# Reordering the products, the first loads and the weight sums of a seven-product projection stage

## The chip, the cores and the metric

One Trainium2 chip, one core. The metric is device time of one execution in microseconds (us), lower is better. The kernel before has a median of 1763.17 us over 3 runs, from 1761.24 to 1765.32.

## What is computed

Two independent attention blocks, A (sliding, dilated window) and B (full), each with 2048 rows, width 640 and 32 heads of 20, in float32. The stage around the change is the first product of block A, `x @ wqkv`:

```python
qkv = (x @ wqkv).reshape(B, S, 3, H, Dh)      # x: 1 x 2048 x 640, wqkv: 640 x 1920
# A: each row attends to itself and 7 earlier rows, 2 apart; B: to all rows
# softmax, weighted sum of v, then @ wo; outputs of A and B side by side
```

## The kernel before

Every float32 product is made of three passes on TensorE (PE): each operand is split into a rounded part ("hi", a cast on ScalarE, ACT) and what the rounding left ("lo", a subtraction on VectorE, DVE), and hi x hi, hi x lo and lo x hi are added up in PSUM (`PASSES`, `product`, lines 30 and 397).

**Block A's projection** (`a_steps`, line 687) makes 12 of the 16 row tiles of 128 rows, in six pairs (`ARows`, `XA[0]` to `XA[5]`), against four groups of weight columns of 512, 512, 448 and 448 (`ACols`, `WP[0]` for the first two, `WP[1]` for the last two). The inner size 640 is five chunks of 128.

1. The first pair of pairs, four row tiles, meets column group 0 chunk by chunk, as the chunks arrive from memory: for each k the x chunks are split (`ARows.chunk`), the weight half too (`ACols.half`), and 12 matmuls follow. Then come the same four tiles against column group 1 from weights that are all there, 15 matmuls a tile.
2. All further work is done by `a_quad` (line 426): two row tiles against two column groups at once with seven block products in the place of eight. It needs sums and differences of blocks of x (`ARows.sums`, `second`, addressed by `X.s(n)`) and of blocks of the weights (`ACols.turn`: four DVE operations in place and into the tile `sums`, then two casts and two subtractions; addressed by `W.T(n)`). One quad has 54 matmuls, five PSUM banks of eight in turn (`next_bank`), one copy and adds on ACT and DVE, and four stores to DRAM (`a_store`, three buffers). `XA[0]` and `XA[1]` run it against `WP[1]` first, quads 0 and 1, then `XA[2]` to `XA[5]` against `WP[0]` and `WP[1]` in turn, quads 2 to 9.

**What sets the order.** Each engine runs its instructions in the order in which the program emits them. `a_steps` and `a_quad` are generators: at each `yield` the loop at line 722 counts n up, issues the stores that are due (`tick`) and emits the side work of that n: `WP[1].base` at n = 1, 2; `WP[1].turn` at n = 4, 5; `WP[0].turn` at n = 8, 10; the split of a later pair of x tiles (`base` at n = 12, 16, 24, 32, `sums` and `second` one step later); the copies of weights to DRAM (`keep`); two late weight chunks (`late_w`, loaded at n = 16 and 20, split two steps later); and at n = 9 eight DMAs that write constants to DRAM. Quad 0 has the yields 8 to 11, quad 1 has 12 to 15, quad 2 has 16 to 19. So what n = 8 emits stands on ACT, DVE and the DMA queue of SP (SyncE) between the first and the second section of quad 0. In a quad before the change:

```python
product(b[0], A11, B11, True, True)               # 6 matmuls
act.copy(c[0], b[0])
product(b[1], X.s(2), W.T(2), True, True)         # 6, needs the weight sums
add(c[1], c[0], b[1])
product(b[0], A12 + l1, B21 + W.c[0], False, True)  # 9, into the bank that ACT has read
```

**Loads.** The loads at the head go out from two queues: per chunk, SP issues the weight half and the x chunk of `XA[0]` (128 x 256), and ACT that of `XA[1]`. Each pair's raw x lies in a `vb` tile of which there are two, and the tile `sums` is a third user of them.

Of the kernel before, what the change touches and what calls it, by code (L numbers as in the profile page):

```python
# [9 lines left out]
F32 = mybir.dt.float32  # L10
# [11 lines left out]
KC = 5  # L22
# [43 lines left out]
def attention_pair(ctx, tc, xa, wqk_a, wv_a, wo_a, xb, wqk_b, wv_b, wo_b, oa, ob):  # L66
# [156 lines left out]
    def lo_of(lo, raw, hi):  # L223
        dve.tensor_tensor(lo, raw, hi.bitcast(F32), ALU.subtract)

    class ARows:


        def __init__(self, p):
            self.p = p  # L230
            self.raw = sb.tile([128, KC, 256], F32, tag="vb", bufs=2, name="stg")
            self.rest = None

        def load(self, *ks, e=sp):
            c = slice(self.p * 256, self.p * 256 + 256)
            if ks:
                for k in ks:
                    e.dma_start(self.raw[:, k], xa[k * 128:(k + 1) * 128, c])
            else:
                sp.dma_start(self.raw, xa[:, c].rearrange("(k p) c -> p k c", p=128))  # L240

        def parts(self, u, k, src):
            m = src.shape[1]
            act.copy(u[:, 0, k:k + m], src)
            lo_of(u[:, 1, k:k + m], src, u[:, 0, k:k + m])

# [3 lines left out]
        def chunk(self, k):  # L250
            if self.rest is None:
                self.home()
                self.rest = sb.tile([128, 2, KC // 2, 128], F32R, tag="raw", bufs=2, name="xr")
            if k == KC - 1:
                self.parts(self.u, 6, self.raw[:, k].rearrange("p (t c) -> p t c", t=2))
                return
            self.parts(self.u, k, self.raw[:, k:k + 1, :128])
            self.parts(*((self.u, 4 + k // 2) if k % 2 else (self.rest, k // 2)), self.raw[:, k:k + 1, 128:])

# [14 lines left out]
        def second(self):  # L274
            self.parts(self.u, 8, self.raw[:, :KC - 1].rearrange("p k (t c) -> p (k t) c", t=2))

# [9 lines left out]
    class ACols:  # L286


        def __init__(self, P):
            self.P, self.n = P, AC[2 * P + 1] - AC[2 * P]  # L290
# [18 lines left out]
            self.raw = [sb.tile([128, 2, n], F32, tag=tag, bufs=2 * (P + 1), name="wr") for tag, _ in self.tags for _ in range(2)]  # L309
            self.raw.append(sb.tile([128, 2, n], F32, tag=f"big{2 + P}", bufs=1, name="wr"))  # L310
            self.lo = []
# [7 lines left out]
        def load(self, k, js=range(2)):  # L319
            P = self.P  # L320
            if P == 0:
                for j in js:
                    sp.dma_start(self.raw[k][:, j].rearrange("p (m c) -> p m c", c=128),
                                 wqk_a[4 * j:4 * j + 4, :, k].rearrange("m p c -> p m c"))
                return
            r = self.raw[k].rearrange("p j c -> p (j c)")
            sp.dma_start(r[:, :256].rearrange("p (m c) -> p m c", c=128), wqk_a[8:10, :, k].rearrange("m p c -> p m c"))
            for h in range(2):
                sp.dma_start(r[:, 256 + h * 320:576 + h * 320], wv_a[h, :, k])

# [17 lines left out]

        def turn(self, kp, x):

            ev, od = self.raw[2 * kp:2 * kp + 2]
            x = x[:, :, :self.n]
            dve.tensor_tensor(x[:, 0], ev[:, 1], ev[:, 0], ALU.subtract)
            dve.tensor_tensor(x[:, 1], od[:, 1], ev[:, 1], ALU.subtract)
            dve.tensor_tensor(od[:, 1], od[:, 1], x[:, 0], ALU.subtract)
            dve.tensor_tensor(od[:, 0], od[:, 0], od[:, 1], ALU.subtract)
            self.lo.append([None, None])
            for o, r in ((1, od), (0, x)):
                self.lo[kp][o] = sb.tile([128, 2, self.n], F32R, tag=self.tags[kp][0], bufs=self.tags[kp][1], name="wl")
                act.copy(self.t[kp][o], r)  # L360
                lo_of(self.lo[kp][o], r, self.t[kp][o])
# [64 lines left out]
    def a_quad(X, W):  # L426
# [10 lines left out]
        act.copy(c[0], b[0])  # L437
        product(b[1], X.s(2), W.T(2), True, True)
        add(c[1], c[0], b[1])
        product(b[0], A12 + l1, B21 + W.c[0], False, True)  # L440
        a_store(g, t, act.copy, b[0])
        yield
        product(b[2], X.s(1), W.T(1), True, True)
        add(c[1], c[1], b[2])
        product(b[3], X.s(4) + l1, B22 + W.c[1], True, True)
        a_store(g + 1, t, add, c[1], b[3])
        yield
        product(b[1], X.s(3), W.T(3), False, True)
        add(c[0], c[0], b[1])
        product(b[4], A22 + l2, W.T(4) + W.c[0], True, True)  # L450
        a_store(g, t + 1, add, c[0], b[4])
        yield
        product(b[2], l2, W.c[1], False, True)
        a_store(g + 1, t + 1, add, c[0], b[2])
        yield
# [12 lines left out]

    XA = [ARows(p) for p in range(2)]
    WP = [ACols(0), ACols(1)]  # L470
    for k in range(KC):
        WP[0].load(k, (0,))
        XA[0].load(k)
        XA[1].load(k, e=act)
    for k in range(KC):
# [246 lines left out]
    for n, _ in enumerate(a_steps()):  # L722
        tick()
        if n == 0:
            for j in range(2):
                WP[1].half(KC - 1, j)
        elif n in (1, 2):
            WP[1].base(n - 1)
        elif n == 3:
            sums = sb.tile([128, 2, 512], F32, tag="vb", bufs=2, name="sums")  # L730
        elif n in (4, 5):
            WP[1].turn(n - 4, sums)
        elif n in (8, 10):
            WP[0].turn(n // 2 - 4, sums)
        if n in (5, 12, 14, 21):
# [4 lines left out]
        elif n in (13, 17, 25, 33):  # L740
            XA[n // 8 + 1].sums()
            XA[n // 8 + 1].second()
        if n == 9:
            for c in range(4):
                sp.dma_start(kb_d[c, 2 * DH:].rearrange("t h (s c) -> (t h) s c", c=128),
                             neg.unsqueeze(1).to_broadcast([64, 4, 128]))
            for u in (ka_d, va_d):
                for hf in range(2):
                    sp.dma_start(u[hf, :PAD].rearrange("p (b c) -> p b c", c=128),
                                 zero.unsqueeze(1).to_broadcast([PAD, KC, 128]))  # L750
        if n in (3, 4) or n > 9 and n % 2 and keeps:
            P, k, j = keeps.pop(0)
            WP[P].keep(k, j)
        if n in (16, 20):
            k = n // 2 - 8
            late_w = [sb.tile([128, WP[1].n], t, tag="aq", bufs=2, name="wt") for t in (F32, F32R)]
            sp.dma_start(late_w[0][:, :128], wv_a[0, :, k, 192:])
            sp.dma_start(late_w[0][:, 128:], wv_a[1, :, k])
        elif n in (18, 22):
            act.copy(late_w[1], late_w[0])  # L760
            lo_of(late_w[0].bitcast(F32R), late_w[0], late_w[1])
            late_w = [late_w[1], late_w[0].bitcast(F32R)]
        elif n in (19, 23):
            k = n // 2 - 9
            WP[1].b12 = {k // 2: late_w}
            WP[1].keep(k, 1)
# [233 lines left out]
    P = {}  # L1000
# [424 lines left out]
```

## Time and profile before

| | us |
|---|---|
| median of 3 runs | 1763.17 |
| lowest, highest | 1761.24, 1765.32 |
| the profiled execution, its own time | 1762.97 |
| its span (first to last instruction) | 1761.2 |
| PE busy in the span | 1738.2 (99%) |
| DVE, ACT, POOL busy | 1417.0, 1335.5, 1228.7 |

Times in the trace are counted from the start of the span. PE is the matmul engine, PEld its weight loads, SPq and ACTq the DMA issues of SyncE and ScalarE. A row of the timeline gives start, duration (of all that are merged in it), engine, operation, output<-inputs, count, and in brackets the idle time before it with what ended it. Tiles have the program's names: `wr` raw weights, `wc`, `wt` their split parts, `wl` lo parts of the weight sums, `stg` raw x, `xn` and `xr` split x, `sum` the two accumulators of a quad (c[0], c[1]), `ro` a result on its way to DRAM, `ps_st` PSUM.

### The profile page before, as it was taken

What the parts mean: (1) busy time and instruction counts of PE and PEld (TensorE: products, weight loads), DVE (VectorE), ACT (ScalarE), POOL (GpSimd) and SP (SyncE); (2) the same over time, 40 slices, a digit from 0 to 9 for tenths busy, and PEclk for the clock granted to TensorE, in tenths of its full rate; (3) what the DMA queues carried; (4) which work ended last, traced back from release to release, by engine and by line L of the source; (5) the groups of instructions that cost most, each with busy time, mean ns of one, the idle gap of its engine ahead of it and who ended that gap; (6) DMA issues with size and microseconds to landing.
All of it is one profiled execution on the core that took longest, in us unless ns stands there. A gap on an engine that the chain in (4) does not pass through costs nothing.

```text
span 1761.2 us, 32060 instructions
## 1 busy us (share of the span) xinstructions
PE 1738.2 (99%) x11271; PEld 990.1 (56%) x11271; DVE 1417.0 (80%) x1948; ACT 1335.5 (76%) x2605; POOL 1228.7 (70%) x1086
## 2 busy tenths in 40 slices
PE   8999999999999999999999999999999999999999
PEld 7888888774444444444444444544444444444569
DVE  7655323689999999999999999999999999999400
ACT  5223222129899999999999999899999999989881
POOL 0000693595988888888899798988888898745442
PEclk9999999999999999999999999999999999999999
DMA  7567967774536554644474455536542634222123
GB/s 227 177 207 252 332 247 258 247 221 113 160 104 175 148 150 128 159 132 141 149 178 143 122 152 152 160 105 173 151 149 90 159 111 132 60 70 69 55 71 111
DMA packets 221496, 270.19 MB, mean 153 GB/s; under 512 B 92812, under 2 KB 142616, under 8 KB 221336
## 3 DMA queue, kind: packets, MB, share of 16 engines
q1 hardware_dynamic: 220040, 266.85, 50.7%
q8 instruction: 88, 1.44, 0.4%
q10 hardware_dynamic: 1296, 1.31, 0.2%
q14 instruction: 72, 0.59, 0.1%
HBM read 193.33 MB, written 74.74 MB: 152 GB/s over the span
## 4 chain that ended last, share of the span: by engine, by line
PE 84%; POOL 4%; DMA 3%; DVE 2%; ACT 2%; issue 1%; SPq 1%; DVEq 0%; POOLq 0%; ACTq 0%
PE ps_st L61 84%; POOL akv L61 2%; DVE mx L61 2%; ACT e L61 1%; DMA stg<-xb 1%; POOL braw L61 1%; SPq L61 1%; DMA bq<-qb_d 1%; DMA stg<-wv_b 0%; ACT more L61 0%; DMA stg<-wo_a 0%; POOL xn L61 0%; POOL al L61 0%; DMA qb_d<-pr 0%; DMA ot_b<-braw 0%
## 5 line engine op out<-in xcount | busy, mean ns | idle before, releaser
L61 DVE TENSOR_REDUCE mx<-ps_st 128x1 f32<-128x512 f32 (+1 forms) x1500 | 1217.8, 878 | 77.2 <-PE ps_st L61 65.8
L61 ACT ACTIVATE e<-ps_st 128x512 f32<-128x512 f32 x2048 | 1067.0, 608 | 36.2 <-PE ps_st L61 16.1
L61 PE MATMUL ps_st<-bq,bk 62*128 62x512 f32 x2048 | 610.9, 439 | 0.2
L61 PE MATMUL ps_st<-bk,bq 60*128 60x512 f32 x2048 | 557.0, 435 | 4.2 <-DVE mx L61 2.1
L61 PEld LDWEIGHTS ps_st<-bq,bk 62*128 62x128 f32 x2048 | 287.9, 184 | 478.6 <-ACT e L61 336.5
L61 PE MATMUL ps_st<-e,vb 128*32 128x512 f32 x4096 | 542.8, 604 | 2.8 <-DVE mx L61 0.4
L61 POOL TENSOR_TENSOR braw<-braw,more 128x512 f32<-128x512 f32 x224 | 288.3, 1287 | 146.9 <-ACT more L61 141.1
L61 POOL TENSOR_TENSOR akv<-akv 128x640 f32<-128x640 f32 (+3 forms) x304 | 282.9, 931 | 23.8
L61 PEld LDWEIGHTS ps_st<-bk,bq 60*128 60x128 f32 x2048 | 264.8, 184 | 37.9 <-DVE mx L61 13.4
L61 POOL TENSOR_TENSOR akv<-akv,aq 128x1280 f32<-128x1280 f32 x64 | 188.2, 2940 | 25.4 <-DMA akv<-ka_d 25.3
L61 PEld LDWEIGHTS ps_st<-e,vb 128*32 128x32 f32 x4096 | 81.9, 108 | 157.3 <-issue 70.8
L61 POOL TENSOR_TENSOR akv<-akv,al 128x1280 f32<-128x1280 f32 x64 | 152.2, 2378 | 0.2
L61 PE MATMUL ps_st<-wc,xn 128*128 128x512 f32 (+1 forms) x544 | 136.5, 384 | 7.7 <-ACT sum L61 4.8
L61 ACT COPY ro<-ps_st 128x320 f32<-128x320 f32 (+2 forms) x102 | 45.9, 452 | 122.8 <-PE ps_st L61 114.9
L61 ACT COPY more<-ps_st 128x512 f32<-128x512 f32 x224 | 132.6, 592 | 2.2 <-PE ps_st L61 1.4
L61 PE MATMUL ps_st<-ww,xn 128*128 128x320 f32 x768 | 125.8, 314 | 0.5 <-ACT e L61 0.5
L61 PEld LDWEIGHTS ps_st<-ww,xn 128*128 128x128 f32 x768 | 113.5, 188 | 20.8 <-ACT e L61 8.8
L61 PEld LDWEIGHTS ps_st<-wc,xn 128*128 128x128 f32 x544 | 103.9, 191 | 24.4 <-ACT sum L61 5.9
L61 PE MATMUL ps_st<-xn,w 128*128 128x512 f32 x480 | 115.6, 389 | 0.3 <-DVE xn L61 0.3
L61 POOL MEMSET ve<- 128x347 f32 x4 | 1.4, 389 | 159.4 <-DVE ro L61 159.4
L61 PEld LDWEIGHTS ps_st<-xn,w 128*128 128x128 f32 x480 | 90.0, 188 | 19.4 <-DVE xn L61 0.7
L61 ACT CAST pr<-ps_st 128x512 fp32r<-128x512 f32 x40 | 23.5, 588 | 89.6 <-PE ps_st L61 89.6
(89 smaller groups left out, 1121.6 us busy)
## 6 DMA issues: line engine op xcount, KB each, us to landing
akv<-ka_d SPq DMA_DIRECT2D x128, 320.0 KB
akv<-va_d SPq DMA_DIRECT2D x128, 320.0 KB
wx<-wa_d SPq DMA_DIRECT2D x24, 480.0 KB
kb_d<-pr SPq DMA_DIRECT2D x20, 512.0 KB
qb_d<-pr SPq DMA_DIRECT2D x20, 512.0 KB
bk<-kb_d SPq DMA_DIRECT2D x16, 640.0 KB
bq<-qb_d SPq DMA_DIRECT2D x64, 160.0 KB
rb<-s_d SPq DMA_DIRECT2D x128, 64.0 KB
```

The costliest lines, as they stand in the source:

```text
L61: return self.tc.keep_in_program_order(op(*a, **k))
```

## The change

The order of the products in a quad changes: the first product, then `b[3]` and the second part of `b[0]`, which need x sums but no weight sums, then those with `W.T`; `b[4]` comes last. `ACols.turn` is split into `sums` (DVE) and `second` (casts, subtractions), which are emitted one step apart. The first x chunks of `XA[0]` and `XA[1]` come as one 128 x 512 load for each k from SP into one tile, in the space that later holds `WP[1]`'s split weights (`big2`), so the two `vb` tiles are free from the start. In odd chunks the two x blocks are split by one operation on each engine. The constants go to DRAM at n = 33 and 35, and the two late weight chunks are split four steps after their load.

```diff
@@ -226,23 +226,17 @@
     class ARows:
 
 
-        def __init__(self, p):
-            self.p = p
+        def __init__(self, p, raw=None):
+            self.p, self.raw, self.rest = p, raw, None
+
+        def load(self):
             self.raw = sb.tile([128, KC, 256], F32, tag="vb", bufs=2, name="stg")
-            self.rest = None
-
-        def load(self, *ks, e=sp):
-            c = slice(self.p * 256, self.p * 256 + 256)
-            if ks:
-                for k in ks:
-                    e.dma_start(self.raw[:, k], xa[k * 128:(k + 1) * 128, c])
-            else:
-                sp.dma_start(self.raw, xa[:, c].rearrange("(k p) c -> p k c", p=128))
+            sp.dma_start(self.raw, xa[:, self.p * 256:self.p * 256 + 256].rearrange("(k p) c -> p k c", p=128))
 
         def parts(self, u, k, src):
-            m = src.shape[1]
-            act.copy(u[:, 0, k:k + m], src)
-            lo_of(u[:, 1, k:k + m], src, u[:, 0, k:k + m])
+            to = k if isinstance(k, slice) else slice(k, k + src.shape[1])
+            act.copy(u[:, 0, to], src)
+            lo_of(u[:, 1, to], src, u[:, 0, to])
 
         def home(self):
             self.u = big(self.p % 2, [128, 2, 16, 128], "xn")
@@ -254,8 +248,12 @@
             if k == KC - 1:
                 self.parts(self.u, 6, self.raw[:, k].rearrange("p (t c) -> p t c", t=2))
                 return
-            self.parts(self.u, k, self.raw[:, k:k + 1, :128])
-            self.parts(*((self.u, 4 + k // 2) if k % 2 else (self.rest, k // 2)), self.raw[:, k:k + 1, 128:])
+            if k % 2:
+                n = 4 + k // 2
+                self.parts(self.u, slice(k, n + 1, n - k), self.raw[:, k].rearrange("p (t c) -> p t c", t=2))
+            else:
+                self.parts(self.u, k, self.raw[:, k:k + 1, :128])
+                self.parts(self.rest, k // 2, self.raw[:, k:k + 1, 128:])
 
         def base(self):
             self.home()
@@ -272,7 +270,10 @@
             dve.tensor_tensor(a12, a12, a11, ALU.subtract)
 
         def second(self):
-            self.parts(self.u, 8, self.raw[:, :KC - 1].rearrange("p k (t c) -> p (k t) c", t=2))
+            hi, lo = (self.u[:, i, 8:].rearrange("p (k t) c -> p k t c", t=2) for i in range(2))
+            src = self.raw[:, :KC - 1].rearrange("p k (t c) -> p k t c", t=2)
+            act.copy(hi, src)
+            lo_of(lo, src, hi)
 
         def rows(self, t, k):
             if t and k % 2 == 0 and k < KC - 1:
@@ -286,7 +287,7 @@
     class ACols:
 
 
-        def __init__(self, P):
+        def __init__(self, P, end):
             self.P, self.n = P, AC[2 * P + 1] - AC[2 * P]
             n = self.n
             if P == 0:
@@ -307,7 +308,7 @@
                 self.b11, self.odd, self.t, self.e = [], [], [], e
             self.c = [[lambda i, j=j: self.last[j][i]] for j in range(2)]
             self.raw = [sb.tile([128, 2, n], F32, tag=tag, bufs=2 * (P + 1), name="wr") for tag, _ in self.tags for _ in range(2)]
-            self.raw.append(sb.tile([128, 2, n], F32, tag=f"big{2 + P}", bufs=1, name="wr"))
+            self.raw.append(end)
             self.lo = []
 
         def home(self, kp):
@@ -323,10 +324,16 @@
                     sp.dma_start(self.raw[k][:, j].rearrange("p (m c) -> p m c", c=128),
                                  wqk_a[4 * j:4 * j + 4, :, k].rearrange("m p c -> p m c"))
                 return
-            r = self.raw[k].rearrange("p j c -> p (j c)")
-            sp.dma_start(r[:, :256].rearrange("p (m c) -> p m c", c=128), wqk_a[8:10, :, k].rearrange("m p c -> p m c"))
-            for h in range(2):
-                sp.dma_start(r[:, 256 + h * 320:576 + h * 320], wv_a[h, :, k])
+            r = self.raw[k]
+            sp.dma_start(r[:, 0, :256].rearrange("p (m c) -> p m c", c=128), wqk_a[8:10, :, k].rearrange("m p c -> p m c"))
+            if k < KC - 1:
+                r = r.rearrange("p j c -> p (j c)")
+                for h in range(2):
+                    sp.dma_start(r[:, 256 + h * 320:576 + h * 320], wv_a[h, :, k])
+                return
+            sp.dma_start(r[:, 0, 256:], wv_a[0, :, k, :192])
+            sp.dma_start(r[:, 1, :128], wv_a[0, :, k, 192:])
+            sp.dma_start(r[:, 1, 128:], wv_a[1, :, k])
 
         def one(self, u, raw):
             act.copy(u[0], raw)
@@ -346,7 +353,7 @@
             self.one(self.b11[kp], self.raw[2 * kp][:, 0])
             self.one(self.odd[kp], self.raw[2 * kp + 1])
 
-        def turn(self, kp, x):
+        def sums(self, kp, x):
 
             ev, od = self.raw[2 * kp:2 * kp + 2]
             x = x[:, :, :self.n]
@@ -354,8 +361,11 @@
             dve.tensor_tensor(x[:, 1], od[:, 1], ev[:, 1], ALU.subtract)
             dve.tensor_tensor(od[:, 1], od[:, 1], x[:, 0], ALU.subtract)
             dve.tensor_tensor(od[:, 0], od[:, 0], od[:, 1], ALU.subtract)
+
+        def second(self, kp, x):
+
             self.lo.append([None, None])
-            for o, r in ((1, od), (0, x)):
+            for o, r in ((1, self.raw[2 * kp + 1]), (0, x[:, :, :self.n])):
                 self.lo[kp][o] = sb.tile([128, 2, self.n], F32R, tag=self.tags[kp][0], bufs=self.tags[kp][1], name="wl")
                 act.copy(self.t[kp][o], r)
                 lo_of(self.lo[kp][o], r, self.t[kp][o])
@@ -435,23 +445,23 @@
         c = [sb.tile([128, 512], F32, tag=tag, bufs=2, name="sum")[:, :n] for tag in ("raw", "rb")]
         product(b[0], A11, B11, True, True)
         act.copy(c[0], b[0])
-        product(b[1], X.s(2), W.T(2), True, True)
-        add(c[1], c[0], b[1])
+        product(b[3], X.s(4) + l1, B22 + W.c[1], True, True)
         product(b[0], A12 + l1, B21 + W.c[0], False, True)
         a_store(g, t, act.copy, b[0])
         yield
+        product(b[1], X.s(2), W.T(2), True, True)
+        add(c[1], c[0], b[1])
         product(b[2], X.s(1), W.T(1), True, True)
         add(c[1], c[1], b[2])
-        product(b[3], X.s(4) + l1, B22 + W.c[1], True, True)
         a_store(g + 1, t, add, c[1], b[3])
         yield
         product(b[1], X.s(3), W.T(3), False, True)
         add(c[0], c[0], b[1])
+        product(b[2], l2, W.c[1], False, True)
+        a_store(g + 1, t + 1, add, c[0], b[2])
+        yield
         product(b[4], A22 + l2, W.T(4) + W.c[0], True, True)
         a_store(g, t + 1, add, c[0], b[4])
-        yield
-        product(b[2], l2, W.c[1], False, True)
-        a_store(g + 1, t + 1, add, c[0], b[2])
         yield
 
     def store_rows(p, dst):
@@ -466,12 +476,12 @@
     banks = all_banks()
 
 
-    XA = [ARows(p) for p in range(2)]
-    WP = [ACols(0), ACols(1)]
+    r = [sb.tile([128, 7, 512], F32, tag=f"big{n}", bufs=1, name="wr") for n in (2, 3)]
+    XA = [ARows(p, r[0][:, 2:, p * 256:p * 256 + 256]) for p in range(2)]
+    WP = [ACols(0, r[0][:, :2]), ACols(1, r[1][:, :2, :448])]
     for k in range(KC):
         WP[0].load(k, (0,))
-        XA[0].load(k)
-        XA[1].load(k, e=act)
+        sp.dma_start(r[0][:, 2 + k], xa[k * 128:(k + 1) * 128, :512])
     for k in range(KC):
         WP[0].load(k, (1,))
     for k in (4, 0, 1, 2, 3):
@@ -727,11 +737,17 @@
         elif n in (1, 2):
             WP[1].base(n - 1)
         elif n == 3:
-            sums = sb.tile([128, 2, 512], F32, tag="vb", bufs=2, name="sums")
-        elif n in (4, 5):
-            WP[1].turn(n - 4, sums)
+            x_sums = sb.tile([128, 2, 512], F32, tag="vb", bufs=2, name="sums")
+            WP[1].sums(0, x_sums)
+        elif n == 4:
+            WP[1].second(0, x_sums)
+            WP[1].sums(1, x_sums)
+        elif n == 5:
+            WP[1].second(1, x_sums)
         elif n in (8, 10):
-            WP[0].turn(n // 2 - 4, sums)
+            WP[0].sums(n // 2 - 4, x_sums)
+        elif n in (9, 11):
+            WP[0].second(n // 2 - 4, x_sums)
         if n in (5, 12, 14, 21):
             XA.append(ARows(len(XA)))
             XA[-1].load()
@@ -740,28 +756,28 @@
         elif n in (13, 17, 25, 33):
             XA[n // 8 + 1].sums()
             XA[n // 8 + 1].second()
-        if n == 9:
-            for c in range(4):
+        if n in (33, 35):
+            for c in range(n - 33, n - 31):
                 sp.dma_start(kb_d[c, 2 * DH:].rearrange("t h (s c) -> (t h) s c", c=128),
                              neg.unsqueeze(1).to_broadcast([64, 4, 128]))
             for u in (ka_d, va_d):
-                for hf in range(2):
+                for hf in range(n // 2 - 16, n // 2 - 15):
                     sp.dma_start(u[hf, :PAD].rearrange("p (b c) -> p b c", c=128),
                                  zero.unsqueeze(1).to_broadcast([PAD, KC, 128]))
         if n in (3, 4) or n > 9 and n % 2 and keeps:
             P, k, j = keeps.pop(0)
             WP[P].keep(k, j)
-        if n in (16, 20):
-            k = n // 2 - 8
+        if n in (16, 24):
+            k = n // 4 - 4
             late_w = [sb.tile([128, WP[1].n], t, tag="aq", bufs=2, name="wt") for t in (F32, F32R)]
             sp.dma_start(late_w[0][:, :128], wv_a[0, :, k, 192:])
             sp.dma_start(late_w[0][:, 128:], wv_a[1, :, k])
-        elif n in (18, 22):
+        elif n in (20, 28):
             act.copy(late_w[1], late_w[0])
             lo_of(late_w[0].bitcast(F32R), late_w[0], late_w[1])
             late_w = [late_w[1], late_w[0].bitcast(F32R)]
-        elif n in (19, 23):
-            k = n // 2 - 9
+        elif n in (21, 29):
+            k = n // 4 - 5
             WP[1].b12 = {k // 2: late_w}
             WP[1].keep(k, 1)
         if n in (34, 37):
```

## Rows read from the trace of the kernel before

**Rows 1.** Busy time of each engine over the span, the page's first part

```profile
PE 1738.2 (99%) x11271; PEld 990.1 (56%) x11271; DVE 1417.0 (80%) x1948; ACT 1335.5 (76%) x2605; POOL 1228.7 (70%) x1086
```

**Rows 2.** Windows, quads 0 and 1: us, busy time by engine, granted clock, DMA

```profile
38.60:50.90 12.30, 11.27 (x55) 9.87 (x54) 9.81 (x13) 5.72 (x8) 0.00 (x0) 1.00 0.40 131
50.90:67.10 16.20, 12.84 (x55) 11.33 (x54) 10.96 (x20) 5.13 (x8) 0.00 (x0) 0.89 0.59 182
```

**Rows 3.** Timeline of PE, the matmuls of quads 0 to 4 that waited

```profile
41.13 0.47 PE L61 MATMUL ps_st<-wl,xn 128*128 128x448 f32 x1 [0.38 <-DVE wl L61]
...
42.25 2.50 PE L61 MATMUL ps_st<-wc,xn 128*128 128x448 f32 x11 [0.65 <-ACT sum L61]
...
56.83 3.37 PE L61 MATMUL ps_st<-wc,xn 128*128 128x448 f32 x11 [3.36 <-ACT sum L61]
...
94.02 2.79 PE L61 MATMUL ps_st<-wc,xn 128*128 128x512 f32 x11 [0.77 <-ACT sum L61]
```

**Rows 4.** Window after the longest wait, granted clock third from the end

```profile
59.00:60.00 1.00, 1.00 (x5) 0.87 (x3) 0.04 (x1) 0.47 (x2) 0.00 (x0) 0.50 0.17 51
```

**Rows 5.** Timeline of ACT around the copies that PE waits for

```profile
41.66 0.54 ACT L61 COPY sum<-ps_st 128x448 f32<-128x448 f32 x1
...
54.35 1.04 ACT L61 CAST wc<-wr 128x1024 fp32r<-128x1024 f32 x1 [6.81 <-DVE wr L61]
...
56.25 0.53 ACT L61 COPY sum<-ps_st 128x448 f32<-128x448 f32 x1
```

**Rows 6.** Timeline of DVE, the x sums, quad 0's first add and the weight sums

```profile
17.72 1.79 DVE L61 TENSOR_TENSOR stg<-stg 128x256 f32<-128x256 f32 x4
...
41.18 1.09 DVE L61 TENSOR_TENSOR wl<-sums,wc 128x896 fp32r<-128x896 f32 x1
42.23 0.62 DVE L61 TENSOR_TENSOR sum<-sum,ps_st 128x448 f32<-128x448 f32 x1
42.77 1.28 DVE L61 TENSOR_TENSOR sums<-wr 128x512 f32<-128x512 f32 x2
...
46.62 1.23 DVE L61 TENSOR_TENSOR wl<-wr,wc 128x1024 fp32r<-128x1024 f32 x1 [1.12 <-ACT wc L61]
...
51.58 1.28 DVE L61 TENSOR_TENSOR sums<-wr 128x512 f32<-128x512 f32 x2
```

**Rows 7.** Timeline of the head, ACT's issues and first work, PE's first product

```profile
0.74 5.09 ACTq L61 DMA_DIRECT2D stg<-xa  x5
...
5.86 1.28 ACT L61 ACT_TABLE_LOAD   x1 [5.86 <-DMA stg<-xa]
...
8.62 0.80 PE L61 MATMUL ps_st<-wc,xn 128*128 128x512 f32 x1 [2.94 <-ACT wc L61]
...
15.66 1.37 ACT L61 CAST wc<-wr 128x512 fp32r<-128x512 f32 x2 [0.18 <-DMA wr<-wqk_a]
```

**Rows 8.** Windows of the head; the last two numbers are DMA share, GB/s

```profile
3.00:8.00 5.00, 2.67 (x13) 2.27 (x11) 0.52 (x3) 2.13 (x6) 0.00 (x0) 1.00 1.05 335
8.00:12.00 4.00, 3.38 (x8) 2.71 (x9) 3.78 (x13) 4.00 (x17) 0.00 (x0) 1.00 0.83 240
12.00:16.00 4.00, 4.00 (x15) 3.18 (x15) 4.00 (x12) 3.71 (x9) 0.00 (x0) 1.00 1.14 345
```

**Rows 9.** Timeline of PE, runs of matmuls without a wait

```profile
45.40 2.39 PE L61 MATMUL ps_st<-wc,xn 128*128 128x448 f32 x11
...
69.87 2.65 PE L61 MATMUL ps_st<-wc,xn 128*128 128x512 f32 x11
```

**Rows 10.** Timeline of ACT and DVE at quad 2's first yield

```profile
72.16 0.59 ACT L61 COPY ro<-ps_st 128x512 f32<-128x512 f32 x1 [2.87 <-PE ps_st L61]
...
73.29 1.36 DVE L61 TENSOR_TENSOR xn<-stg,xn 128x512 fp32r<-128x512 f32 x3 [2.46 <-ACT xn L61]
74.57 0.68 DVE L61 TENSOR_TENSOR sum<-sum,ps_st 128x512 f32<-128x512 f32 x1
```

**Rows 11.** Timeline of SP's queue, half of the constants of n = 9

```profile
50.86 2.62 SPq L61 DMA_DIRECT2D kb_d<-neg  x4
```

## The prediction

> **What bounds the kernel now.** I read the page's busy times first: PE works in 99% of the span [rows 1], so the run ends when PE ends, and only time in which PE waits, or runs at a lower clock, can be won. The windows say where that is. In quads 0 and 1 PE is busy for 11.27 of 12.30 us and 12.84 of 16.20 us, and in the second the mean granted clock is 0.89 [rows 2]. Next PE's timeline: three waits in quads 0 and 1, of 0.38, 0.65 and 3.36 us, and one of 0.77 in quad 4 [rows 3]. After the longest, the clock stands at 0.50, the 1.2 GHz level [rows 4]; a mean of 0.89 over 16.20 us is 1.8 us of PE time lost to it. At the head PE idles 2.94 us until the first real product at 8.62 [rows 7]. All of it is 0.38 + 0.65 + 3.36 + 0.77 + 1.8 = 7.0 us in the quads, and the head's wait.
>
> Then I asked what ends the longest wait. It is named after ACT's copy `sum` at 56.25, into which ACT goes straight from two weight casts; the first of these stood idle for 6.81 us waiting for DVE's weight sums [rows 5]. DVE's timeline shows why those were late: x sums from 17.72, the last subtraction for `WP[1]` at 41.18 to 42.27, the sums of the first half of `WP[0]` from 42.77, the second half from 51.58, with idle gaps of about 1.1 us where it waits for a cast [rows 6]. So the quads wait for **a chain of DVE and ACT work that starts at 17.72 and is nearly without slack**; the order of the products is the last link only. A change helps as far as it starts this chain earlier, shortens it, or gives PE less to do behind it.
>
> **The change, part by part.** The sum is made against the profiled execution, 1762.97 us (span 1761.2), which is 0.20 below the median.
>
> *Head.* ACT loses its five DMA issues, 5.09 us from 0.74, after which its table load ran from 5.86 to 7.14 [rows 7]. The first x chunk now lies behind one weight half: 512 KB at 335 GB/s [rows 8] from 3.0 land near 4.6. From the end of the table load to the first product took 1.48 us, so it now comes at 6.1 if the load is done by then, at 7.4 if the load again waits for data: 1.2 to 2.5 us of PE earlier. I count none of it: quad 0 reaches its second part of `b[0]` earlier and waits there for the copy `sum`, which stands on ACT behind the casts of the chain.
>
> *Start of the chain.* The x sums follow the last weight half of the head, whose cast waited for data at 15.66 [rows 7]. Ahead of its end lie 15 loads of 256 KB, 3.93 MB. Memory moved 335 GB/s from 3 to 8 us and 345 from 12 to 16, but 240 between [rows 8]. With rows of 2 KB in place of 1 KB in SP's queue I take the dip as mostly gone: 3.93 MB at 340 GB/s are 11.6 us, to 14.6 in place of about 16.3. The two engines also save four short operations each. I take **-1.5**; the ends are -1.9, and +1.5 if one queue only keeps the 265 GB/s that 3.93 MB from 3.0 to 17.8 would mean.
>
> By the Trainium skill, "DMA: Bandwidth & Descriptors", section "Issuing engines are not separate DMA queues", DMAs issued on several engines run on the same 16 DMA engines, and issuing them concurrently only saves the sequencer's issue time. By that alone the data would land when it did, and the sum below would be +0.7 in place of -0.9; the dip to 240 is what speaks for more.
>
> *The chain itself.* `sums` one step ahead of `second` leaves DVE's order for `WP[1]` as it was: sums, two subtractions, sums, two subtractions. From the copy `sum` at 41.66 to 42.20 [rows 5], now 40.7: 9 matmuls and then 6 at 0.203 us each (2.39 less 0.36 over ten [rows 9]) end at 43.8. DVE is done with `WP[1]` at 42.27 - 1.5 = 40.8, runs the four sums of `WP[0]` (42.77 to about 45.5 before [rows 6]) to 43.5, waits for that product, and adds from 44.0 to 44.6; two more adds of 0.6 behind the product that ends at 45.0 bring it to 46.4, two subtractions of 1.2 to 48.8, two adds to 50.0, four sums to 52.7. Two casts on ACT, 54.35 to 56.25 before [rows 5], end at 54.6, the copy at 55.1, and PE goes on at 55.2 in place of 56.83: **-1.6**. The new wait in the chain (DVE for the first product) takes the place of the old one at 46.62 [rows 6].
>
> *Less behind it.* When that copy comes PE has 39 matmuls of quad 1 left, not 42: 3 x 0.203 = **-0.6**. The pause ahead of it is about as long as before, so I leave the 1.8 us of low clock as they are; without it, another -1.8.
>
> *New waits.* At the first yield the first add (`c[1]`) is not yet emitted. Behind the yields of n = 16, 24 and 32 it now stands on DVE behind three subtractions for the next x pair, which end at 74.57, and takes 0.68 [rows 10]: until 75.25. The third product into the same bank, 12 matmuls of 0.226 after 71.9 (nine into the run that starts at 69.87 [rows 9]), could start at 74.6. That is 0.6 for each of quads 2, 4 and 6: **+1.8**, between 0 and 2.1. In quad 1 the low clock covers it. Quad 2's x split stands one add of 0.62 [rows 6] later against PE: **+0.3**, between 0 and 0.6.
>
> *Late weights and constants.* The wait of 0.77 in quad 4 [rows 3] was a copy behind a cast of late weights; with four steps in place of two it goes: **-0.8**. The eight DMAs of constants leave n = 9 (four took 2.62 us of SP's time [rows 11]) for n = 33 and 35. There they hold up stores and one load by about 3 us at a time, covered by three store buffers and by the steps between a load and its use; without that cover, up to 3 us.
>
> *The rest.* From quad 10 on nothing changes but the start; PE is 99% busy, so I pass the sum on whole.
>
> Sum: -1.6 - 0.6 + 1.8 + 0.3 - 0.8 = -0.9, so **1762.1 us**. A measurement of this kernel can tell about 0.2%, 3.5 us, from no change; this is less.
>
> **The rivals.**
>
> *The waits go.* If the earlier head and the new order let PE pass quads 0 and 1 without waiting, the 7.0 us go, with 1.2 at the head: 8.2, so 1754.8. For it: 24 matmuls, 4.9 us, now stand ahead of the first weight sum in each quad, where there were six. Against it: the copy is on ACT behind the casts as before, and DVE had only gaps of some 1.1 us. It would need the chain about 5 us earlier.
>
> *A second fall of the clock (slower).* PE comes to quad 0's copy up to 3 us earlier, and the copy hardly earlier: a pause of some 3 us, like the one that the 0.50 followed [rows 3, 4]. It decides if that pause brings the clock down and the data of the head comes no earlier. Then the products of quad 0 that DVE adds up run at half speed: 1.8 us more in the chain in place of -1.5, and the add held up in quad 1 too (0.6): -0.9 + 1.5 + 1.8 + 0.6 = +3.0, and with 1.5 for loads that come late on one queue +4.5: 1767.5.
>
> The Trainium skill, "TensorE: Matmul & The Clock Gate", section "HAM oscillation — how this bites in real kernels", has the array throttled again after a wait for data, each time anew; rows 3 and 4 agree for the one pause here.
>
> *One queue changes nothing.* Data lands as before, the chain starts at 17.72: -0.9 + 1.6 = +0.7, 1763.7. This is also what comes out if the first-chunk edit does not do what it says.
>
> **How the numbers follow.** My forecast 0.45, one queue changes nothing 0.22, the waits go 0.19, the second fall 0.14. The first two both lie within 0.2%, and nearly all that I leave uncertain in them stays there: same 0.66, faster 0.20 (with a little of the forecast, where the pause no longer lowers the clock), slower 0.14. The likeliest case alone spans 1759.5 (chain at -1.9, low clock gone) to 1765.5 (chain at +1.5). For 8 in 10 the range takes part of the faster rival: 1757.0 to 1766.5.
>
> **What would show it.** Right: first product between 6 and 7.5; x sums on DVE near 16.2; PE waiting in quad 0 for ACT's `sum`, and again some 3 us in quad 1 until about 55; DVE almost without gaps between; 0.6 us waits for DVE `sum` in quads 2, 4 and 6; none of ACT in quad 4; block B's first product near 160. Wrong: no wait over 1 us in quads 0 and 1, x sums before 15 or after 18, or a wait over 1 us between 100 and 200.

## The result, and the profile after

The changed kernel takes 1768.24 us (median of 20 runs, 1765.49 to 1771.94), the kernel before 1762.50 beside it (20 runs, 1760.37 to 1765.35): ratio 1.0032, 95% interval 1.0025 to 1.0039. It is **slower by 0.32%, 5.7 us**; the forecast was 1762.1, range 1757.0 to 1766.5. The profiled execution took 1765.75 (span 1764.0), 2.5 below its median; that of before lay 0.5 above its own, so the two traces differ by only 2.8 in all. The stage is therefore measured where it ends, at block B's first product. Timeline of PE before, then after (start, duration, form, count, wait):

```profile
161.04 2.91 PE L61 MATMUL ps_st<-xn,w 128*128 128x512 f32 x12
```

```profile
6.31 0.79 PE L61 MATMUL ps_st<-wc,xn 128*128 128x512 f32 x1 [0.63 <-ACT wc L61]
...
42.99 4.47 PE L61 MATMUL ps_st<-wc,xn 128*128 128x448 f32 x11 [4.17 <-ACT sum L61]
...
60.01 2.54 PE L61 MATMUL ps_st<-wc,xn 128*128 128x448 f32 x11 [3.49 <-ACT sum L61]
...
65.24 0.68 PE L61 MATMUL ps_st<-wc,xn 128*128 128x448 f32 x2 [0.63 <-DVE sum L61]
...
77.20 0.39 PE L61 MATMUL ps_st<-wl,xn 128*128 128x512 f32 x1
78.10 0.73 PE L61 MATMUL ps_st<-wc,xn 128*128 128x512 f32 x2 [0.51 <-DVE sum L61]
...
102.27 0.73 PE L61 MATMUL ps_st<-wc,xn 128*128 128x512 f32 x2 [0.52 <-DVE sum L61]
...
126.44 0.73 PE L61 MATMUL ps_st<-wc,xn 128*128 128x512 f32 x2 [0.52 <-DVE sum L61]
...
150.75 0.74 PE L61 MATMUL ps_st<-wc,xn 128*128 128x512 f32 x2 [0.81 <-DVE sum L61]
...
165.91 2.97 PE L61 MATMUL ps_st<-xn,w 128*128 128x512 f32 x12
```

Block B starts 4.9 us later. From there to the end the changed kernel's trace is 2.1 shorter than the other (1598.1 us for 1600.2), which leaves the 2.8; the account below is of the 4.9, and what the median of 5.7 has beyond it these two traces do not show. The head is won, 6.31 for 8.62 [rows 7], and so is quad 4's 0.77 [rows 3]. The waits of 0.38, 0.65 and 3.36 have become 4.17 and 3.49, and there are five new ones on DVE's add, from quad 1 on. Windows of after (columns as in [rows 2, 8]):

```profile
3.00:8.00 5.00, 4.37 (x17) 3.67 (x16) 1.59 (x5) 1.41 (x5) 0.00 (x0) 1.00 0.86 266
8.00:12.00 4.00, 4.00 (x13) 3.15 (x13) 3.22 (x10) 3.54 (x11) 0.00 (x0) 1.00 1.11 344
12.00:16.00 4.00, 4.00 (x19) 3.29 (x18) 3.73 (x8) 3.33 (x7) 0.00 (x0) 1.00 1.20 291
38.60:50.90 12.30, 8.13 (x30) 7.13 (x29) 7.58 (x11) 5.61 (x8) 0.00 (x0) 0.72 0.43 138
50.90:67.10 16.20, 12.07 (x58) 10.47 (x57) 12.95 (x20) 4.08 (x7) 0.00 (x0) 1.00 0.40 128
67.10:161.00 93.90, 91.55 (x419) 77.79 (x418) 46.70 (x77) 19.89 (x34) 0.72 (x2) 1.00 0.67 214
43.00:48.00 5.00, 5.00 (x13) 4.45 (x14) 2.69 (x5) 1.20 (x2) 0.00 (x0) 0.50 0.29 100
```

The 1.2 GHz level has moved: quad 1 has none (1.00 for 0.89), quad 0 has it from its pause on (0.50 from 43 to 48, mean 0.72). The profile's record of the clock starts at 10.5 us here and at 13.8 in the trace before; the 1.00 of the windows ahead of that is no reading. Timelines of DVE, then ACT, then SP's queue:

```profile
18.45 1.80 DVE L61 TENSOR_TENSOR wr<-wr 128x256 f32<-128x256 f32 x4
...
48.70 0.62 DVE L61 TENSOR_TENSOR sum<-sum,ps_st 128x448 f32<-128x448 f32 x1 [2.90 <-PE ps_st L61]
...
54.76 1.29 DVE L61 TENSOR_TENSOR sums<-wr 128x512 f32<-128x512 f32 x2
```

```profile
0.73 1.28 ACT L61 ACT_TABLE_LOAD   x1 [0.73 <-PEq L1427]
...
17.19 0.62 ACT L61 CAST wc<-wr 128x512 fp32r<-128x512 f32 x1 [0.26 <-DMA wr<-wqk_a]
...
42.40 0.55 ACT L61 COPY sum<-ps_st 128x448 f32<-128x448 f32 x1
...
59.43 0.52 ACT L61 COPY sum<-ps_st 128x448 f32<-128x448 f32 x1
```

```profile
5.76 1.99 SPq L61 DMA_DIRECT2D wr<-xa  x1
7.80 5.57 SPq L61 DMA_DIRECT2D wr<-wqk_a  x6
```

The chain starts at 18.45, not 17.72 [rows 6]: the last weight half's cast still waits for data at 17.19. In quad 0 DVE stands idle for 2.90 us for products that run at 1.2 GHz, so the sums of `WP[0]`'s second half come at 54.76, not 51.58 [rows 6], and the copy at 59.43, not 56.25 [rows 5].

**The account to block B's start.** Copy in quad 1: 60.01 - 56.83 = +3.2. Three matmuls fewer behind it: -0.6. Low clock in quad 1: -1.8. Waits on the add: +4.7 (below). Quad 4's wait of 0.77, counted from start to start: 94.02 - 69.87 = 24.15 us [rows 3, 9] for the 23.17 of two quads without a wait (next paragraph), -1.0. Sum +4.5, of +4.9.

**A wait costs more than its bracket.** At quad 2's, one matmul starts at 77.20 and the next at 78.10, 0.90 where 0.226 is the step [rows 9]: 0.67 lost. From quad 2's wait to quad 4's it is 102.27 - 78.10 = 24.17 us, where 54 x (0.226 + 0.203) = 23.17 are two quads without one. So a "0.51" costs 0.7 to 1.0; I take 0.9 for each of quads 1, 2, 4 and 6 and 1.1 for quad 8 (0.81): 4.7.

### The profile page after: what moved, and what is told of

Same layout as the page of the kernel before. It is cut to its first block, busy times and chain, and to the rows that moved or that the text cites. A ratio compares the mean times of both kernels' runs of the same rounds, so it can differ in the third digit from the quotient of the medians.

```text
span 1764.0 us, 32040 instructions
## 1 busy us (share of the span) xinstructions
PE 1739.4 (99%) x11271; PEld 990.3 (56%) x11271; DVE 1417.4 (80%) x1944; ACT 1335.2 (76%) x2601; POOL 1229.2 (70%) x1086
## 4 chain that ended last, share of the span: by engine, by line
PE 88%; DVE 3%; DMA 2%; ACT 2%; issue 1%; POOL 0%; SPq 0%; DVEq 0%; ACTq 0%
PE ps_st L61 88%; DVE mx L61 2%; ACT e L61 1%; DMA stg<-xb 1%; DMA bq<-qb_d 1%; DMA stg<-wo_a 1%; DVE xn L61 0%; DMA stg<-wv_b 0%; ACT xn L61 0%; ACT more L61 0%; SPq L61 0%; DVE sum L61 0%; ACT ro L61 0%; POOL ww L61 0%; DVE mtr L61 0%
```

## Experiments

My theory after the result had three parts: **(a)** the new order holds PE up at the first add, which now stands behind a yield's side work on DVE; **(b)** the early head only lengthens the pause in quad 0, the clock falls there, and the slow products delay DVE's chain; **(c)** the chain starts 0.7 later, as the last weight halves do. The rival was that one part is all of it. Every ratio is to the kernel before, run beside it on the same chip; its median was 1762.83 for the first four kernels, 1762.99 for the next four and 1763.25 for the last two.

**Fill the pauses (b).** Each of quads 0 and 1 computes its first product three more times into a bank that is written anew later; nothing uses them.

```diff
         product(b[3], X.s(4) + l1, B22 + W.c[1], True, True)
+        if W.P and X.p < 2:
+            for _ in range(3):
+                product(b[1], A11, B11, True, True)
```

> The changed kernel, with three extra copies of the first product (18 matmuls, about 3.7 us, into a bank that the next product overwrites) ahead of the point where PE pauses in quad 0 (4.17 us) and quad 1 (3.49 us). Theory 'clock': the pauses bring PE to half clock, in quad 0 the 15 slow matmuls feed DVE's adds and delay the whole chain by 2.4 us, and in many runs the second pause does it again. Then PE that works through both pauses keeps its clock: no window at 0.5 in the quads, quad 1 goes on near 57.5 in place of 60.0, 4 us faster than the changed kernel, about 1764, and little spread. Rival 'head' (x sums on DVE at 18.45 in place of 17.72) and rival 'adds' (new waits of PE for DVE adds, 0.63 + 0.51 + 0.52 + 0.52 + 0.81 us): no gain, 1768 or a little more.

Measured: 1765.3, before 1762.83, ratio 1.0014 (1.0005 to 1.0023): some 3 us less than the change, with 36 matmuls more. Timeline of PE and the window of quad 0:

```profile
42.49 2.50 PE L61 MATMUL ps_st<-wc,xn 128*128 128x448 f32 x11 [1.93 <-ACT sum L61]
...
163.09 2.96 PE L61 MATMUL ps_st<-xn,w 128*128 128x512 f32 x12
```

```profile
38.60:50.90 12.30, 10.37 (x51) 9.30 (x50) 9.81 (x13) 5.72 (x8) 0.00 (x0) 1.00 0.49 154
```

The clock stays up and block B starts 2.8 earlier. Of this 0.5 is not the clock's: in this trace the x sums start at 17.95, in the change's at 18.45, with the same loads. The low clock in quad 0 is worth the other 2.3 us, near the 2.4 by which the slow products hold up the chain (worked out below), and does not explain the rest.

**The old order of products, with all else of the change (a).**

```diff
-        product(b[3], X.s(4) + l1, B22 + W.c[1], True, True)
+        product(b[1], X.s(2), W.T(2), True, True)
+        add(c[1], c[0], b[1])
...
```

> The changed kernel with the order of products of before. Theory 'clock': PE still gets to quad 0 about 2.6 us early and pauses there some 3 us for the weight sums, the clock falls in quad 0, and the chain behind it is late: 1766 to 1768. Rival 'adds': the 3.0 us of new waits go, 1765. Rival 'head': the chain starts 0.7 late, so 1763 to 1764.

Measured: 1763.76, ratio 1.0012 (1.0001 to 1.0022), 4.5 below the change. Timeline of PE, and the window of quads 2 to 9:

```profile
40.50 0.68 PE L61 MATMUL ps_st<-wc,xn 128*128 128x448 f32 x2 [4.20 <-ACT wc L61]
...
42.74 4.48 PE L61 MATMUL ps_st<-wc,xn 128*128 128x448 f32 x11 [0.38 <-ACT sum L61]
...
59.82 2.50 PE L61 MATMUL ps_st<-wc,xn 128*128 128x448 f32 x11 [3.45 <-ACT sum L61]
...
161.26 2.91 PE L61 MATMUL ps_st<-xn,w 128*128 128x512 f32 x12
```

```profile
67.10:161.00 93.90, 93.90 (x439) 82.13 (x438) 49.58 (x82) 21.36 (x36) 0.72 (x2) 1.00 0.69 223
```

The pause and the slow products of quad 0 stay; the waits on the add go, and 4.65 us with them (165.91 - 161.26). The order costs that after the 0.6 that it wins behind the copy; PE leaves quad 1's pause 0.2 earlier here (59.82 for 60.01), so the waits alone are worth 4.65 + 0.6 - 0.2, some 5.1, where the account has 4.7. With 5.1 in it the account comes to +4.9. The expectation from the clock alone, 1766 to 1768, missed.

**The new order alone, on the kernel before (a without b and c).** Its edit is the part of the change in `a_quad`.

```diff
-        product(b[1], X.s(2), W.T(2), True, True)
-        add(c[1], c[0], b[1])
+        product(b[3], X.s(4) + l1, B22 + W.c[1], True, True)
...
```

> The kernel before with only the new order of products. Theory 'clock': PE starts late as before, the pause in quad 0 is under 1 us, no fall of the clock there; quad 1 as before with 3 matmuls less behind its pause: -0.6, and the adds' waits of about 2 us in quads 2 to 8: 1763.5 to 1764.5. Rival 'adds' alone explains the change: +3.0 at least and more, 1766 to 1768. Rival 'head': 1762.

Measured: 1765.33, ratio 1.0018 (1.0008 to 1.0028).

```profile
49.35 0.68 PE L61 MATMUL ps_st<-wc,xn 128*128 128x448 f32 x2 [2.46 <-DVE sum L61]
...
57.38 2.49 PE L61 MATMUL ps_st<-wc,xn 128*128 128x448 f32 x11 [1.07 <-ACT sum L61]
...
163.82 2.97 PE L61 MATMUL ps_st<-xn,w 128*128 128x512 f32 x12
```

In its timeline of PE quad 0 now holds 2.46 of the pause that quad 1 had, and quad 1 has 1.07 left; the clock does not fall in either quad, yet block B starts 2.8 later. The time lies between what the theory (1763.5 to 1764.5) and its rival (1766 to 1768) had expected: the theory took the waits at 2, which is too little.

**The old head, with the new order; the new head alone (b, c).**

```diff
-    XA = [ARows(p, r[0][:, 2:, p * 256:p * 256 + 256]) for p in range(2)]
+    XA = [ARows(p, sb.tile([128, KC, 256], F32, tag="vb", bufs=2, name="stg")) for p in range(2)]
...
-        sp.dma_start(r[0][:, 2 + k], xa[k * 128:(k + 1) * 128, :512])
+        for x, e in zip(XA, (sp, act)):
+            e.dma_start(x.raw[:, k], xa[k * 128:(k + 1) * 128, x.p * 256:x.p * 256 + 256])
```

> The changed kernel with the first x chunks loaded as before, two 128 x 256 loads for each k from two queues into the vb tiles. Theory 'clock': first product again near 8.6, no long pause in quad 0, clock 1.00 there; 1763 to 1764. Rival 'head' in its other form (the chain starts 0.73 later because of the one queue): only 0.7 us better than the changed kernel, 1767.5. Rival 'adds': 1768.

Measured: 1766.92, ratio 1.0023 (1.0013 to 1.0033), nearer to its rival's 1767.5 than to the theory's 1763 to 1764.

```profile
163.66 2.92 PE L61 MATMUL ps_st<-xn,w 128*128 128x512 f32 x12
```

Block B starts 2.25 before the change's. Quad 0's pause is gone (0.57), but the low clock is back in quad 1, behind a wait of 3.44, and the waits on the add remain. The second kernel is the one before with the change's loads, their one tile and the merged split of odd chunks, and nothing else of it:

```diff
-        XA[0].load(k)
-        XA[1].load(k, e=act)
+        sp.dma_start(r[0][:, 2 + k], xa[k * 128:(k + 1) * 128, :512])
```

> The kernel before with only the new head: the first x chunks as one 128 x 512 load for each k from SP, into one tile, and one split operation in odd chunks. Theory: x sums start some 0.5 to 0.7 us later, PE reaches quad 0 about 2.5 us early and pauses there 3 to 4 us, the clock falls in quad 0 and the chain is 2 us late, while the pause in quad 1 is as before: +1 to +3 against the kernel before, 1764 to 1766. Rival, that an earlier head is worth its 2.3 us: 1760.5. Rival, that it changes nothing: 1762.8.

Measured: 1764.27, before 1762.99, ratio 1.0012 (1.0002 to 1.0022). Its timelines of PE and DVE:

```profile
6.54 0.50 PE L61 MATMUL ps_st<-wc,xn 128*128 128x512 f32 x1 [0.87 <-ACT wc L61]
...
40.80 1.11 PE L61 MATMUL ps_st<-wc,xn 128*128 128x448 f32 x2 [4.20 <-ACT wc L61]
...
161.82 2.91 PE L61 MATMUL ps_st<-xn,w 128*128 128x512 f32 x12
```

```profile
18.51 1.80 DVE L61 TENSOR_TENSOR wr<-wr 128x256 f32<-128x256 f32 x4
```

A head 2 us earlier does not help: the pause in quad 0 grows from 0.4 + 0.65 to 4.2, the x sums come 0.8 late without any of the rest, and so does block B. In old_head's trace the x sums start at 17.40. Over all traces they start at 17.95 to 18.51 in the seven with the new loads and at 17.40 to 18.05 in the five with the old: (c) belongs to the loads, and its 0.7 is some tenths more or less from run to run.

**The add ahead of the yield, in quads 2 to 9 (a).**

```diff
+        if X.p < 2:
+            yield
         product(b[1], X.s(2), W.T(2), True, True)
         add(c[1], c[0], b[1])
+        if X.p > 1:
+            yield
```

> The changed kernel, in quads 2 to 9 with the first yield behind the add into c[1] in place of ahead of it, so that the add stands ahead of the side work on DVE. Theory 'adds': the waits of 0.51, 0.52, 0.52 and 0.81 us in quads 2, 4, 6 and 8 go and nothing takes their place: -2.4 against the changed kernel, 1765.8. Rival: another add behind the side work takes over (b[2] waits for its reader in the same way) and at most 0.5 is won: 1767.7.

Measured: 1767.02, ratio 1.0025 (1.0013 to 1.0037), only 1.2 below the change. The waits went but for small rests (window of quads 2 to 9: PE 93.89 of 93.90, with 432 matmuls where the old order has 439), and block B starts at 163.06, 2.9 earlier. But this profile has a longer pause in quad 0, and the low clock in quad 1 too. Its restart in quad 0, and the window of the head:

```profile
42.58 4.25 PE L61 MATMUL ps_st<-wc,xn 128*128 128x448 f32 x11 [5.55 <-ACT sum L61]
```

```profile
8.00:12.00 4.00, 4.00 (x19) 3.34 (x18) 3.68 (x11) 3.54 (x11) 0.00 (x0) 1.00 1.11 347
```

PE comes to this pause at 37.03, in the change's trace at 38.82, and the chain starts only 0.41 earlier (18.04): so the pause is 1.4 longer. The 1.8 are won at the head, where PE starts 19 matmuls between 8 and 12 us; in the change's trace it starts 13, 0.43 apart until 10.3.

**The copy ahead of the casts.** All these traces share one thing: ACT's copy `sum` stands behind two casts that wait for DVE. Here the casts and subtractions of each second weight half are emitted behind that copy, inside quads 0 and 1.

```diff
         act.copy(c[0], b[0])
+        if W.P and X.p < 2:
+            WP[1 - X.p].second(1, x_sums)
...
-        elif n == 5:
-            WP[1].second(1, x_sums)
```

> The changed kernel with the second halves of the weight casts emitted inside quads 0 and 1, behind ACT's copy sum, in place of ahead of it. Theory 'ACT order': the pauses of 4.2 and 3.5 us at the copy go, shorter waits of PE for the weight sums and for an add (0.3 to 0.5 and 2 to 3 us in quad 0, 1 to 2 us in quad 1) take their place, the clock stays at 1.00 in the quads: -6 to -8 against the changed kernel, 1760 to 1762. Rival 'DVE chain': PE is held by the DVE work whatever stands on ACT, the pauses only move: 1766 to 1768.

Measured: 1762.95, ratio 1.0000 (0.9991 to 1.0010): 5.3 below the change, though 1 us short of the 1760 to 1762 expected. The waits on the add are still there. The next kernel also takes the add in all quads ahead of the yield, and `b[4]` ahead of `b[2]` as before:

```diff
-        yield
         product(b[1], X.s(2), W.T(2), True, True)
         add(c[1], c[0], b[1])
+        yield
...
```

> As copy_first, and in all quads the first yield behind the first add, and b[4] ahead of the second part of b[2] as in the kernel before. Theory: the add's waits go too; what is left are waits of 0.3 us in quad 0, some 3 us in quad 1 and 1.5 us at the start of quad 2: 1757.5 to 1759.5, 3 to 5 us faster than the kernel before. Rival: the DVE chain gives the time back in longer waits in quads 1 and 2: 1762.

Measured: **1757.66** (5 runs, 1756.53 to 1758.35), ratio 0.9970 (0.9957 to 0.9982): faster than both kernels. Timeline of ACT and of PE:

```profile
36.73 0.54 ACT L61 COPY sum<-ps_st 128x448 f32<-128x448 f32 x1
39.25 0.94 ACT L61 CAST wc<-wr 128x896 fp32r<-128x896 f32 x1 [1.98 <-DVE wr L61]
```

```profile
37.33 2.50 PE L61 MATMUL ps_st<-wc,xn 128*128 128x448 f32 x11 [0.57 <-ACT sum L61]
...
57.53 0.97 PE L61 MATMUL ps_st<-wc,xn 128*128 128x448 f32 x2 [3.08 <-DVE sum L61]
...
155.68 2.98 PE L61 MATMUL ps_st<-xn,w 128*128 128x512 f32 x12
```

The copy comes at 36.73, not 42.40, and quad 0 starts its nine matmuls 5.7 earlier; the one long wait left is on DVE's add in quad 1. How the gain over the kernel ahead of it divides between the add and `b[4]` was not tested.

**The same edit on the kernel before, and the old head under the best version.** The first puts the line `WP[1 - X.p].second(1, sums)` behind the copy in the kernel before; the second is the edit of the old head above, made to the kernel of 1757.66.

> The kernel before with one edit only: in quads 0 and 1 the two casts and subtractions of the second weight half stand behind ACT's copy `sum`, not ahead of it. Theory (the bound is the place of the copy on ACT; neither the order of the products nor the head is needed for a gain): PE's wait in quad 1, 3.36 us, moves to DVE's first add or the lo parts of the weights, and some of it goes; 1758 to 1761, ratio 0.9975 to 0.999. Rival (the copy's place pays only where products without weight sums stand behind it, as in the changed order; here the second product needs the weight sums anyway): the wait only changes its name from ACT sum to DVE wl or ACT wc at the second product, and the time stays within 0.1% of before.

> copy_first_order with the first x chunks again as two 128x256 loads from SP's and ACT's queues. Theory (the early head only moves PE's wait into quad 0 and delays the weight chain by 0.7 us): the first product comes near 8.4, x sums near 17.8, and the time is within 0.1% of copy_first_order's 1757.7 or up to 1 us below it. Rival (with the copy out of the way, PE can use the 2.3 us that the early head gives): 1 to 2.3 us more than copy_first_order, 1758.7 to 1760.

Measured: 1759.21, ratio 0.9987 (0.9976 to 0.9999); and 1759.59, ratio 0.9981 (0.9973 to 0.9990). Block B's start in the first, then in the second:

```profile
158.25 2.91 PE L61 MATMUL ps_st<-xn,w 128*128 128x512 f32 x12
```

```profile
158.60 2.92 PE L61 MATMUL ps_st<-xn,w 128*128 128x512 f32 x12
```

So the place of the copy alone gains 2.8 us to block B without any other part of the change, though the ratio is barely clear of 1. The early head seems to be worth 2 to 3 us once the copy is out of the way (block B 155.68 for 158.60; the ratios' intervals overlap by a little). That was the rival of the last expectation, and the theory there, that the early head only moves the wait, missed. The x sums of the two traces start at 17.96 and 18.05, so this gain is not in the chain's start.

## Why the prediction was wrong

- **Start of the chain, -1.5: wrong.** It was +0.7 (18.45). 3 to 8 us moved 266 GB/s for 335 [rows 8], 12 to 16 moved 291 for 345; only the dip was filled, as forecast (344 for 240). SP issues all loads now, and its queue stood for 1.99 us at one load and took 5.57 for the last six weight halves, which had taken 4.80:

```profile
8.53 4.80 SPq L61 DMA_DIRECT2D wr<-wqk_a  x6
```

That the x sums started after 18 was one of the prediction's own signs of being wrong. By the rule of the Trainium skill that the prediction set against this term ("DMA: Bandwidth & Descriptors", "Issuing engines are not separate DMA queues") alone there was nothing to gain; the trace agrees that nothing was gained, and has a loss beside it.
- **The low clock left "as they are": wrong.** The prediction saw PE pause in quad 0, but ran the 15 products behind the pause at 0.203. They ran at half the clock (11 in 4.47 us) and DVE waited 2.90 for them: the chain lost about 2.4 there, 15 x 0.203 = 3.05 against the 5.46 from 42.99 to 48.45, where the 16th starts. With the start, 2.2 + 2.4 = 4.6 of the 4.8 by which PE missed the 55.2 at which it was to go on in quad 1 (60.01). In quad 1 the clock did not fall, which gave back the 1.8 that the sum had left in.
- **New waits, +1.8: right in place, too small, and the largest miss of the sum.** Those of quads 2, 4 and 6 came as described (0.51, 0.52, 0.52), quad 1's 0.63 was taken as covered by a low clock that was not there, quad 8's was not looked for, and a wait costs 0.9 or more, not its bracket: 4.7, and some 5.1 by the experiment with the old order.
- **Right:** first product 6.31 (6 to 7.5); PE waiting in quad 0 for ACT's `sum`; quad 4's wait gone; three matmuls fewer behind the copy. The +0.3 for quad 2's x split did not show: PE has no wait for `xn` there. The constants at n = 33 and 35 show no wait of PE.
- **The rival that came in** is "a second fall of the clock", 1767.5 at 0.14. Its mechanism is the one shown (products of quad 0 at half speed in the chain, an add that holds quad 1 up as well, data no earlier); it came out 0.7 low. That it came so near is in part luck: it has a start 0.8 later than the measured one and 1.8 of low clock in quad 1 that was not there, and these make up for waits that are too small there too. Its point of decision (a pause that brings the clock down, with data no earlier) could have had more weight: the prediction's own views had the pause and the row of 0.50 side by side. One sum is off: the terms named for the ends of the likeliest case give 1759.9 and 1765.1, not 1759.5 and 1765.5; the range does not hang on it.

What stays open: the changed kernel's executions range over 6 us with mean clocks from 0.998 (1765.75) down to 0.995 (1771.94), and only one of the fastest was profiled. Where the others lost the clock was not seen. Four other traces (old_head, only_head, add_first, copy_first) show one more place: a fall near 318 us, in block B, where PE waits for the loads of `bq`. They take 1600.4 to 1603.3 us from block B's start to the end, the other eight 1597.2 to 1600.2. So in old_head and add_first the gain at block B's start does not show whole in the time. One such window, of old_head:

```profile
322.00:324.00 2.00, 2.00 (x8) 2.00 (x8) 2.00 (x2) 0.43 (x1) 0.00 (x0) 0.50 0.70 244
```

Why the new loads bring the last weight halves later is open too.

## What to carry to other kernels

When an edit brings an engine earlier to a wait whose end does not move, it buys only a longer pause, and the pause can be paid twice: once at the clock, and again if the slowed products feed the chain that is being waited for. Look first at what stands ahead of the releasing instruction on its in-order engine: moving one copy ahead of two waiting casts gained what reordering the products could not. An add or copy that frees a bank goes ahead of a yield's side work, and a wait of half a microsecond that recurs in every second loop turn is counted by the period between its occurrences.

## What the runs showed of the hardware that was not expected

- The length of a pause did not decide whether the clock fell. It fell after the waits of 3.36 [rows 3, 4], 3.08 (the kernel of 1757.66) and 2.82 us (copy_first), and not after 3.49 (the change, quad 1), 3.45 (the old order, quad 1) and 2.88 (the old head under the best version). The Trainium skill's account of a clock that throttles after a wait for data ("TensorE: Matmul & The Clock Gate", "HAM oscillation — how this bites in real kernels") agrees with the falls; these rows show that not every such wait brings one. Windows at four of these waits: copy_first, copy_first_order, the change, copy_first_order_old_head:

```profile
46.35:50.90 4.55, 4.55 (x15) 4.10 (x16) 4.27 (x6) 1.44 (x2) 0.00 (x0) 0.62 0.14 50
```

```profile
57.60:61.60 4.00, 4.00 (x12) 3.59 (x13) 3.86 (x9) 0.00 (x0) 0.00 (x0) 0.57 0.87 269
```

```profile
59.50:61.00 1.50, 0.99 (x5) 0.93 (x6) 1.40 (x2) 0.45 (x2) 0.00 (x0) 1.00 0.74 245
```

```profile
60.00:64.00 4.00, 3.69 (x18) 3.42 (x19) 3.86 (x9) 0.00 (x0) 0.00 (x0) 1.00 0.76 239
```

- The activation table load started at 0.73 without waiting for data; before, it stood behind ACT's five DMA issues until 5.86 [rows 7].
- The head's first products ran at the 1.2 GHz level wherever the old head made PE wait 2.7 to 3.4 us for the first weights: in all five traces with it they start 0.43 apart, as at the head of the change's own trace, against 0.23 in the other six with the new head. Where the record of the clock reaches back that far it says 0.50; the new order alone, from 8 to 12 us:

```profile
8.00:12.00 4.00, 3.59 (x9) 2.82 (x10) 3.78 (x13) 4.00 (x16) 0.00 (x0) 0.50 0.83 246
```

- From 12 to 16 us the DMA engines were busier and moved less: a share of 1.20 at 291 GB/s, against 1.14 at 345 [rows 8]. It is not the wider rows of x: nearly all that moved then (2299 of 2300 packets) was in rows under 2 KB, as before. The cause is open.
